# A fused decay-attention and feed-forward kernel: the order of all matmuls written into the source

## The chip, the cores and the metric

One core of a Trainium2 chip runs the whole program. The metric is the device time of one execution in microseconds (us), taken as the median of the runs shown. Engines are named as in the profile: PE is the matrix engine (its weight loads are listed as PEld), DVE the vector engine, ACT the scalar engine, POOL the general one, SP the engine whose queue issues nearly all transfers here.

## The reference: what is computed

A linear attention with a complex decay for each channel, and on its output a two-layer feed-forward net:

```python
mag = np.sqrt(a_re * a_re + a_im * a_im)
scale = np.minimum(mag, 0.999) / (mag + 1e-06)
a_re_n, a_im_n = (a_re * scale, a_im * scale)
for t in range(S):
    new_re = ar * S_re - ai * S_im
    new_im = ar * S_im + ai * S_re
    kv = np.einsum('bhd,bhe->bhde', k[:, :, t], v[:, :, t])
    S_re, S_im = (new_re + kv, new_im)
    y[:, :, t] = np.einsum('bhd,bhde->bhe', q[:, :, t], S_re)
x = y.transpose(0, 2, 1, 3).reshape(B * S, H * D)
h = x @ w_in
out = np.maximum(0.01 * h, h) @ w_out
```

There are 4 batches, 8 heads, 768 positions, a head width of 48; so 3072 tokens of width 384, a hidden width of 2048, all in fp32.

## The kernel before, in words

The sequence is cut into chunks of 128 positions. A **pass** is one chunk of two batches; there are 12 passes (0 to 11), and a pass holds two **units**, one for each batch. The last two passes (10 and 11) are the last chunk of the sequence: they carry no state on and skip the work for it. After each pass its 256 tokens are a **group** (0 to 11) of the feed-forward net.

*Preparing a pass* (`prep`, lines 430 to 603) is DVE and ACT work: the decays are normalised, multiplied up along the chunk (lines 478 to 505), and turned into scaled queries and keys in the tile `qkt`; its last two DVE instructions stand at line 576. Ten transfers on SP's queue (lines 592 to 602) then move `qkt` into the tile `t96` (`t` in the profile). `qkt`, `t96` and the values `v` have one buffer each: the next pass can be moved into `t96` only when the matmuls and scalings that read it for this pass are done.

*Attention of a unit* (`attend`) has these steps on PE. Transposes of the keys (line 635, the tile `kn` after an ACT copy). Scores (line 649), multiplied on DVE with a mask into `asb` (line 657). The output (line 678) from `asb` and `v`, and from the carried state `rst`; ACT and DVE split it into a high and a low part, `xh` and `xl` (lines 680 and 683). The new state (line 692), added on DVE (line 703) and scaled on ACT (line 710, eight instructions). All of them use three PSUM banks in turn.

*The feed-forward net of a group* (`moe`) goes in eight steps of 256 hidden units. Its **first half step** `mm1` is 18 matmuls of 128x256 into the tile `ph` (lines 732 to 734; weights and inputs are split in a high and a low part, and three of the four products are taken). ACT and DVE make the activation and split it: ACT line 738 and DVE line 739 give `tg`, ACT line 740 `gh`, DVE line 741 `gl`. The **second half step** `mm2` is 18 matmuls that add into three tiles `po` (lines 749, 750, 755). `ph` has two buffers, and so have `tg`, `gh` and `gl`. In the source `mm2` of a step stands one step behind `mm1`.

*The weights* arrive as 64-bit words. In the first 156 us they are converted piece by piece on DVE (lines 416 and 420), ACT (423, 425) and POOL (424, 426), 32 pieces, between the preparations of passes 0 to 2. Near the end all weights are read once more and checked on ACT (lines 389 to 396, the tile `wck`).

*What sets the order.* The kernel is written in a framework that records all instructions and, before the program is built, puts those of each engine in one fixed order: it plays the program through with an estimated time for each instruction, and of what is ready takes the one with the lowest priority number. `prio` sets these numbers: attention first, then the feed-forward net, then preparation. So before the change attention and feed-forward matmuls mix on PE as that plan fell out, and the engines then run their lists strictly in order, each instruction waiting for its semaphores.

Of the kernel before, what the change touches and what calls it, by code (L numbers as in the profile page):

```python
# [17 lines left out]
DM = H * D  # L18
# [20 lines left out]
GROUPS = [2] * 12  # L39
GT = max(GROUPS) * C  # L40
GW = max(g * C * max(1, 4 // g) for g in GROUPS)
# [234 lines left out]
def body(ctx, tc, keep, a_in, qk_in, v_in, w_in, out):  # L276
# [23 lines left out]
    wacc = keep.tile([P, 2, WCP * -(-NWC // WCK)], F32, tag="wacc", name="wacc")  # L300

# [314 lines left out]
    def xgroup(u):  # L616
        g = next(g for g in range(len(GROUPS)) if u < sum(GROUPS[: g + 1]))
# [4 lines left out]
        return *xg[g], (u - sum(GROUPS[:g])) * C  # L622

    def attend(n, bi):
        prio(PRIO_ATT)
        c, bs = SUBS[n]
        qkt, t96, v = relay[n]
        for b in bs[bi : bi + 1]:
            xh, xl, x0 = xgroup(SUB_POS[n] // C + bi)
            if c < NCH - 1:  # L630
                kn = pp.tile([P, H, 2, D], F32, tag="kn", name=f"kn_{n}_{bi}")
                for hh in range(2):
                    pt = att_bank()
                    for h4 in range(4):
                        nc.tensor.transpose(  # L635
                            out=pt[:, h4, 0:96],
                            in_=t96[:, slot_of(1, hh * 4 + h4), bi, 0:C],
                            identity=ident[0:96, 0:96],
                        )
                    nc.scalar.copy(  # L640
                        kn[:, hh * 4 : hh * 4 + 4].rearrange("p h l d -> p h (l d)"), pt[:, :, 0:96]
                    )
            am = []
            for hh in range(2):
                ps = att_bank()
                for h4, x in score_order():
                    h = hh * 4 + h4
                    q = block_lane(h4, x)
                    nc.tensor.matmul(  # L649
# [7 lines left out]
                nc.vector.tensor_tensor(  # L657
                    out=asb, in0=ps, in1=mask, op=ALU.mult
                )
                am.append(asb)  # L660
            px = att_bank()
# [14 lines left out]
            for step in zip(*lanes):  # L676
                for q, (i, lhsT, rhs, first, last) in enumerate(step):
                    nc.tensor.matmul(px[32 * q : 32 * q + 32, i], lhsT=lhsT, rhs=rhs, start=first, stop=last)  # L678
            u = SUB_POS[n] // C + bi
# [7 lines left out]
            if c < NCH - 1:  # L687
                pu = att_bank().rearrange("p a b -> p (a b)")
                for h in range(H):
                    o = VW + h * D  # L690
                    for q in range(3):
                        nc.tensor.matmul(
                            pu[32 * q : 32 * q + 32, h * D : (h + 1) * D],
                            lhsT=kn[:, h].rearrange("p l d -> p (l d)")[:, 32 * q : 32 * q + 32],
                            rhs=v[:, bi, o : o + D],
                            start=True,
                            stop=True,
                        )
                u = pu[0:96, 0:DM].rearrange("p (k j e) -> p k j e", j=2, e=D)
                r0 = rst[:, b, 0, 0]  # L700
                r = bass.AP(r0.tensor, r0.offset, [list(r0.ap[0]), [PAIR, H // 2], [64, 2], [1, D]])
                if c > 0:
                    nc.vector.tensor_tensor(out=r, in0=u, in1=r, op=ALU.add)
                src = u if c == 0 else r
                for h0 in (0, 1, 6):
                    hn = 2 if h0 == 6 else 3
                    s0 = slot_of(0, h0)
                    for x in range(hn):
                        h = h0 + (x if h0 == 6 else 2 * x)
                        nc.scalar.activation(  # L710
                            r[:, h // 2, h % 2], src[:, h // 2, h % 2], AF.Copy, scale=t96[:, s0 + x, bi, C : C + 1]
                        )

    def moe(g):
        prio(PRIO_MOE)
        u0 = sum(GROUPS[:g])
        ns = GROUPS[g]
        pos, nt = u0 * C, ns * C
        xh, xl, _ = xgroup(u0)

        po = [pso.tile([P, 512], F32, tag=f"o{o}", name=f"po_{g}_{o}") for o in range(NOC)]

        nf = max(1, 512 // nt)
        w = nf * nt

        def mm1(f0):
            ph = psh.tile([P, 512], F32, tag="h", name=f"ph_{g}_{f0}")
            for f in range(f0, f0 + nf):
                fs = slice(f * P, (f + 1) * P)
                o = ph[:, (f - f0) * nt : (f - f0 + 1) * nt]  # L730
                for k in range(TI):
                    nc.tensor.matmul(o, lhsT=win_hi[:, k, fs], rhs=xh[:, k, :nt], start=(k == 0), stop=False)  # L732
                    nc.tensor.matmul(o, lhsT=win_hi[:, k, fs], rhs=xl[:, k, :nt], start=False, stop=False)  # L733
                    nc.tensor.matmul(o, lhsT=win_lo[:, k, fs], rhs=xh[:, k, :nt], start=False, stop=(k == TI - 1))  # L734
            tg = pp.tile([P, GW], F32, tag="tg", name=f"tg_{g}_{f0}", bufs=2)
            gh = pp.tile([P, GW], F32R, tag="gh", name=f"gh_{g}_{f0}", bufs=2)
            gl = pp.tile([P, GW], F32R, tag="gl", name=f"gl_{g}_{f0}", bufs=2)
            nc.scalar.activation(tg[:, :w], ph[:, :w], AF.Copy, scale=0.01)  # L738
            nc.vector.tensor_tensor(out=tg[:, :w], in0=ph[:, :w], in1=tg[:, :w], op=ALU.max)  # L739
            nc.scalar.copy(gh[:, :w], tg[:, :w])  # L740
            nc.vector.tensor_tensor(out=gl[:, :w], in0=tg[:, :w], in1=gh[:, :w].bitcast(F32), op=ALU.subtract)  # L741
            return gh, gl

        def mm2(f0, gh, gl):
            for f in range(f0, f0 + nf):
                ts = slice((f - f0) * nt, (f - f0 + 1) * nt)
                for o in range(NOC):
                    os = slice(o * P, (o + 1) * P)
                    nc.tensor.matmul(po[o][:, :nt], lhsT=wout_hi[:, f, os], rhs=gh[:, ts], start=(f == 0), stop=False)  # L749
                    nc.tensor.matmul(po[o][:, :nt], lhsT=wout_lo[:, f, os], rhs=gh[:, ts], start=False, stop=False)  # L750
            for f in range(f0, f0 + nf):
                ts = slice((f - f0) * nt, (f - f0 + 1) * nt)
                for o in range(NOC):
                    os = slice(o * P, (o + 1) * P)
                    nc.tensor.matmul(  # L755
                        po[o][:, :nt], lhsT=wout_hi[:, f, os], rhs=gl[:, ts], start=False, stop=(f == NFC - 1)
                    )
# [111 lines left out]
```

## Time and profile before

| what | value |
|---|---|
| median of 3 runs | 689.54 us (688.95 to 689.71) |
| the profiled execution's own time | 694.78 us |
| its span | 692.7 us |
| mean granted clock of PE | 0.959 |
| PE busy | 569.1 us, 82% of the span |
| DVE busy | 550.4 us, 79% |
| ACT busy | 367.4 us, 53% |
| POOL busy | 78.8 us, 11% |

How to read it: the page cuts the span into 40 slices of 17.3 us, with the busy share of each engine in tenths, and the clock that PE was granted. Busy times of PE are modelled ends, so a PE that is shown as busy can still be waiting for a part of that time. A group's row gives the number of its instructions, their summed busy time, the mean of one, and the idle time ahead of them with what ended it. One profiled execution took 5.2 us longer than the median of the runs; all terms of a sum are of that one execution.

### The profile page before, as it was taken

How to read it: one execution, taken by the hardware profiler on the slowest of the kernel's cores; microseconds unless marked ns; L12 is line 12 of the kernel's file. 1: busy time of each engine (PE TensorE's matmuls, PEld its weight loads, DVE VectorE, ACT ScalarE, POOL GpSimd, SP SyncE). 2: the span in 40 equal slices, each digit the busy share in tenths (PEclk: the TensorE clock that was granted, in tenths of full speed). 3: DMA queues.
4: the chain of work that ended last, by engine and by line, in shares of the span. 5: the costliest groups of instructions: out<-in, count | busy, mean ns of one | idle time of the engine just before them, and what ended most of it. 6: DMA issues, size and time to landing. Idle time of an engine off the chain costs nothing.

```text
span 692.7 us, 17741 instructions
## 1 busy us (share of the span) xinstructions
PE 569.1 (82%) x7554; PEld 541.4 (78%) x7554; DVE 550.4 (79%) x917; ACT 367.4 (53%) x827; POOL 78.8 (11%) x75
## 2 busy tenths in 40 slices
PE   1000446999999999999999998999999898799996
PEld 0000335988998899898998998989989888799996
DVE  5999899899979799698897896978979977233332
ACT  6345266358356285283653843836628348584331
POOL 5645355350000000000000000000000000000000
PEclk9999965999999999999999998999999999899999
DMA  9232742722522613416126134170171566870000
GB/s 347 78 102 68 225 146 92 175 102 74 102 84 82 177 51 68 141 53 160 49 68 190 52 70 138 51 185 26 50 206 52 93 234 190 257 261 24 24 1 28
DMA packets 26246, 79.22 MB, mean 114 GB/s; under 512 B 3376, under 2 KB 9520, under 8 KB 26160
## 3 DMA queue, kind: packets, MB, share of 16 engines
q1 hardware_dynamic: 25552, 76.43, 36.7%
q10 hardware_dynamic: 608, 1.59, 1.0%
q8 instruction: 61, 1.00, 0.6%
q14 instruction: 25, 0.20, 0.1%
HBM read 54.26 MB, written 4.72 MB: 85 GB/s over the span
## 4 chain that ended last, share of the span: by engine, by line
DVE 38%; PE 32%; DMA 13%; issue 7%; ACT 4%; SPq 4%; POOL 1%; ACTq 0%; DVEq 0%
DMA t<-qkt 8%; PE po L749 4%; PE ph L734 4%; PE po L750 4%; PE po L755 4%; PE ph L732 4%; PE ph L733 4%; DVE gl L741 3%; PE att L649 3%; DVE tg L739 3%; DMA wck<-in_w_dram 3%; DVE a L530 2%; PE att L678 2%; DVE tmp L481 2%; DVE asb L657 2%
## 5 line engine op out<-in xcount | busy, mean ns | idle before, releaser
L732 PE MATMUL ph<-xh,win_hi 128*128 128x256 f32 x576 | 166.2, 289 | 14.0 <-DVE tg L739 8.6
L733 PE MATMUL ph<-xl,win_hi 128*128 128x256 f32 x576 | 166.4, 289 | 2.6 <-DVE xl L683 2.5
L734 PE MATMUL ph<-xh,win_lo 128*128 128x256 f32 x576 | 165.9, 288 | 0.0
L749 PE MATMUL po<-gh,wout_hi 128*128 128x256 f32 x576 | 147.0, 290 | 1.4 <-ACT gh L740 1.4
L750 PE MATMUL po<-gh,wout_lo 128*128 128x256 f32 x576 | 145.3, 287 | 0.0
L732 PEld LDWEIGHTS ph<-xh,win_hi 128*128 128x128 f32 x576 | 111.4, 194 | 16.3 <-DVE tg L739 10.3
L733 PEld LDWEIGHTS ph<-xl,win_hi 128*128 128x128 f32 x576 | 111.5, 194 | 3.7 <-DVE xl L683 3.1
L749 PEld LDWEIGHTS po<-gh,wout_hi 128*128 128x128 f32 x576 | 111.8, 195 | 3.4 <-ACT gh L740 2.2
L734 PEld LDWEIGHTS ph<-xh,win_lo 128*128 128x128 f32 x576 | 112.1, 195 | 0.5 <-issue 0.4
L750 PEld LDWEIGHTS po<-gh,wout_lo 128*128 128x128 f32 x576 | 111.7, 195 | 0.4
L738 ACT ACTIVATE tg<-ph 128x512 f32<-128x512 f32 x96 | 57.1, 594 | 89.5 <-PE ph L734 79.2
L739 DVE TENSOR_TENSOR tg<-ph,tg 128x512 f32<-128x512 f32 x96 | 65.7, 685 | 48.3 <-ACT tg L738 45.7
L635 PE MATMUL att<-ident,t 96*128 96x96 f32 x160 | 26.9, 272 | 85.5 <-DMA t<-qkt 81.1
L635 PEld LDWEIGHTS att<-ident,t 96*128 96x128 f32 x160 | 16.7, 146 | 94.2 <-DVE a L484 72.5
L755 PE MATMUL po<-gl,wout_hi 128*128 128x256 f32 x576 | 87.5, 286 | 0.2 <-DVE gl L741 0.2
L740 ACT CAST gh<-tg 128x512 fp32r<-128x512 f32 x96 | 59.1, 617 | 48.3 <-DVE tg L739 41.0
L741 DVE TENSOR_TENSOR gl<-tg,gh 128x512 fp32r<-128x512 f32 x96 | 65.8, 688 | 16.4 <-ACT gh L740 14.4
L755 PEld LDWEIGHTS po<-gl,wout_hi 128*128 128x128 f32 x576 | 77.0, 193 | 1.3 <-DVE gl L741 0.4
L657 DVE TENSOR_TENSOR asb<-att,mask 128x512 f32<-128x512 f32 x48 | 32.5, 685 | 39.3 <-PE att L649 39.3
L649 PE MATMUL att<-t 96*32 96x64 f32 (+3 forms) x1536 | 51.6, 267 | 6.0 <-DMA t<-qkt 6.0
L481 DVE TENSOR_TENSOR tmp<-a 128x384 f32<-128x384 f32 x84 | 52.1, 621 | 1.2
L649 PEld LDWEIGHTS att<-t 96*32 96x32 f32 x1536 | 40.2, 147 | 13.9 <-DMA t<-qkt 6.9
(119 smaller groups left out, 938.2 us busy)
## 6 DMA issues: line engine op xcount, KB each, us to landing
t<-qkt SPq DMA_DIRECT2D x44, 290.2 KB, 5.3
wck<-in_w_dram SPq DMA_DIRECT2D x10, 1152.0 KB, 5.6
v<-in_v_dram SPq DMA_DIRECT2D x12, 832.0 KB, 4.4
a<-in_a_dram SPq DMA_DIRECT2D x12, 768.0 KB, 6.1
qk<-in_qk_dram SPq DMA_DIRECT2D x12, 768.0 KB, 4.9
out_dram<-ot SPq DMA_DIRECT2D x12, 384.0 KB, 2.6
stage_xh<-in_w_dram SPq DMA_DIRECT2D x10, 384.0 KB, 3.0
stage_xl<-in_w_dram SPq DMA_DIRECT2D x10, 384.0 KB, 3.6
```

The lines of the kernel that those rows point to most:

```text
L481: nc.vector.tensor_tensor(out=pr, in0=src.unsqueeze(2).to_broadcast([P, 2, 2, M]), in1=swap(ar, r), op=ALU.mult)
L649: nc.tensor.matmul(ps[32 * q : 32 * q + 32, h4].rearrange("p (y x) -> p y x", x=NB)[:, :, x:], lhsT=from_block(t96, 1, h, bi, x, x + 1), r ...
L732: nc.tensor.matmul(o, lhsT=win_hi[:, k, fs], rhs=xh[:, k, :nt], start=(k == 0), stop=False)
L733: nc.tensor.matmul(o, lhsT=win_hi[:, k, fs], rhs=xl[:, k, :nt], start=False, stop=False)
L734: nc.tensor.matmul(o, lhsT=win_lo[:, k, fs], rhs=xh[:, k, :nt], start=False, stop=(k == TI - 1))
L738: nc.scalar.activation(tg[:, :w], ph[:, :w], AF.Copy, scale=0.01)
L739: nc.vector.tensor_tensor(out=tg[:, :w], in0=ph[:, :w], in1=tg[:, :w], op=ALU.max)
L740: nc.scalar.copy(gh[:, :w], tg[:, :w])
L741: nc.vector.tensor_tensor(out=gl[:, :w], in0=tg[:, :w], in1=gh[:, :w].bitcast(F32), op=ALU.subtract)
L749: nc.tensor.matmul(po[o][:, :nt], lhsT=wout_hi[:, f, os], rhs=gh[:, ts], start=(f == 0), stop=False)
L750: nc.tensor.matmul(po[o][:, :nt], lhsT=wout_lo[:, f, os], rhs=gh[:, ts], start=False, stop=False)
L755: nc.tensor.matmul(po[o][:, :nt], lhsT=wout_hi[:, f, os], rhs=gl[:, ts], start=False, stop=(f == NFC - 1))
```

## The change

The matmuls and transposes of attention and of the feed-forward net go through a new helper that tells the framework to keep these instructions on PE in the order of the source. The other engines' orders are still made by the framework.

The order in the source is new. `attend` no longer does its work at once: it returns two pieces for each unit, so four for a pass. The first, `scores`, holds the scores and the first half of the key transposes; the second, `update`, the other half of the transposes, the output and the new state. `moe` is replaced by `first`, `second` and `stream`: `stream` lists the half steps of a group, and `second` of a step now stands two steps behind `first` (after `first` of the step behind next). For groups 2 to 10 the last two `second` half steps are put into the next group's list, behind its `first` of step 0. The main loop walks through the half steps of group n-1 and puts the pieces of pass n between them when few half steps are left (`GAP`, `TAIL`). For passes 1 and 2 `TAIL` is -100, so their four pieces come only when groups 0 and 1 are wholly done. `tg`, `gh` and `gl` get three buffers instead of two.

```diff
+OVERLAP = range(2, 11)
+GAP = 2
+TAIL = [0, -100, -100, 0, 2]
...
+    def mm(out, **kw):
+        tc.keep_in_program_order(nc.tensor.matmul(out, **kw))
...
     def attend(n, bi):
...
+        def turn(hh):
+            pt = att_bank()
...
+            nc.scalar.copy(kn[0][:, hh * 4 : hh * 4 + 4].rearrange("p h l d -> p h (l d)"), pt[:, :, 0:96])
+
+        def scores():
+            prio(PRIO_ATT)
             for hh in range(2):
                 ps = att_bank()
                 for h4, x in score_order():
...
-                    nc.tensor.matmul(
+                    mm(
...
+            if carry:
+                kn.append(pp.tile([P, H, 2, D], F32, tag="kn", name=f"kn_{n}_{bi}"))
+                turn(0)
+
+        def update():
+            prio(PRIO_ATT)
+            if carry:
+                turn(1)
             px = att_bank()
...
+        return [scores, update]
...
-        prev = None
-        for f in range(0, NFC, nf):
-            cur = mm1(f)
-            if prev is not None:
-                mm2(f - nf, *prev)
-            prev = cur
-        mm2(NFC - nf, *prev)
...
+    def first(g, s):
+        prio(PRIO_MOE)
+        xh, xl, _ = xgroup(g * GT // C)
+        ph = psh.tile([P, NF, GT], F32, tag="h", name=f"ph_{g}_{s}")
...
+        tg = pp.tile([P, NF, GT], F32, tag="tg", name=f"tg_{g}_{s}", bufs=3)
+        gh = pp.tile([P, NF, GT], F32R, tag="gh", name=f"gh_{g}_{s}", bufs=3)
+        gl = pp.tile([P, NF, GT], F32R, tag="gl", name=f"gl_{g}_{s}", bufs=3)
...
+    def second(g, s):
...
+    def stream(g):
+
+        late = [(second, g - 1, s) for s in (NS - 2, NS - 1)] if g - 1 in OVERLAP else []
+        order = [(first, g, 0), *late, (first, g, 1), (first, g, 2)]
+        for s in range(3, NS):
+            order += [(second, g, s - 3), (first, g, s)]
+        order += [(second, g, NS - 3)]
+        if g not in OVERLAP:
+            order += [(second, g, s) for s in (NS - 2, NS - 1)]
+        return order
...
+    for n in range(nsub + 1):
+        pieces = []
+        if n < nsub:
+            prep(n, PRIO_PREP + n * 10_000, 1)
...
+            pieces = [p for bi in range(len(SUBS[n][1])) for p in attend(n, bi)]
+        else:
+            check_weights()
+        if n > 0:
+            order = stream(n - 1)
+            for i, (what, g, s) in enumerate(order):
+                what(g, s)
+                left = len(order) - 1 - i
+                while pieces and left <= GAP * len(pieces) + TAIL[min(n, len(TAIL) - 1)]:
+                    pieces.pop(0)()
+                    if left > 0:
+                        break
...
+        for p in pieces:
+            p()
```

**In the program's order, PE, pass 5.** Names with `ph_4_8` belong to group 4 (before the change the second number counts blocks of 128 hidden units, so 8 is step 4; in the changed kernel it counts steps), `asb_5_0_1` is pass 5, unit 0, the second half of the masked scores. Before, in the middle of the first unit:

```order
L678 MATMUL att2_101<-asb_5_0_0_3821,v_5_3112 32x128 x2
L692 MATMUL att0_99<-v_5_3112,kn_5_0_3794 32x48 x24
L755 MATMUL po_4_2_3348<-gl_4_4_3440,wout_hi_75 128x256
L755 MATMUL po_4_0_3346<-gl_4_4_3440,wout_hi_75 128x256
L755 MATMUL po_4_1_3347<-gl_4_4_3440,wout_hi_75 128x256
```

In the changed kernel, the `update` piece of the same unit, between a second and a first half step:

```order
L308 MATMUL po_4_2_3514<-gl_4_1_3481,wout_hi_75 128x256
L647 MATMUL att1_100<-ident_77,t96_5_3374 128x96 x4
L308 MATMUL att2_101<-asb_5_0_0_3549,v_5_2711 32x128 x4
L308 MATMUL att2_101<-t96_5_3374,rst_80 32x128 x4
L308 MATMUL att2_101<-asb_5_0_0_3549,v_5_2711 32x128 x2
L308 MATMUL att2_101<-asb_5_0_1_3567,v_5_2711 32x128 x2
```

Before, the attention of a unit is broken up by single feed-forward matmuls wherever the plan had something ready; now a piece is closed, and it sits behind the second half step of step 1 and ahead of the first half step of step 4.

**In the program's order, DVE, pass 1.** Before, the first masked scores of pass 1 stand between the activations of group 0, in the middle of the conversion of the weights (`wcv`, `stage`):

```order
L739 TENSOR_TENSOR tg_0_8_856<-ph_0_8_837,tg_0_8_856 128x512
L420 SCALAR_TENSOR_TENSOR stage_xh_6_129<-stage_xh_6_129,wcv_29_441 128x384
L416 TENSOR_SCALAR wcv_14_449<-stage_xl_7_130 128x384
L484 TENSOR_TENSOR a_2_1116<-tmp_2_1678 128x2x96
L657 TENSOR_TENSOR asb_1_0_0_1151<-att0_99,mask_78 128x512
L420 SCALAR_TENSOR_TENSOR stage_xl_7_130<-stage_xl_7_130,wcv_14_449 128x384
```

In the changed kernel they stand behind the last `gl` of group 0 and behind half of the preparation of pass 2:

```order
L753 TENSOR_TENSOR tg_0_7_1058<-ph_0_7_1039,tg_0_7_1058 128x512
L533 TENSOR_TENSOR qkt_2_1360<-a_2_756 128x2x768
L469 SCALAR_TENSOR_TENSOR tmp_3_1994<-tmp_3_1994 128x768
L755 TENSOR_TENSOR gl_0_7_1060<-tg_0_7_1058,gh_0_7_1059 128x512
L538 TENSOR_TENSOR a_2_756<-a_2_756 128x1536
L539 TENSOR_TENSOR a_2_756<-a_2_756,qkt_2_1360 128x768
L540 TENSOR_TENSOR a_2_756<-a_2_756,qkt_2_1360 128x768
L475 TENSOR_TENSOR tmp_3_1994<-tmp_3_1994 128x768
L572 TENSOR_TENSOR qkt_2_1360<-qk_2_757,a_2_756 128x6x128
L670 TENSOR_TENSOR asb_1_0_0_1140<-att1_100,mask_78 128x512
```

So the attention of pass 1 moved behind all of group 0 on DVE too. Further on, the second `xl` of pass 1 stands behind the two last instructions of the preparation of pass 2; before, it stood ahead of them, with seven activation instructions of group 1 (four `tg`, three `gl`) in between.

More of the change, by code (lines that the diff above doesn't have):

```diff
@@ L616, in xgroup @@
     def xgroup(u):
-        g = next(g for g in range(len(GROUPS)) if u < sum(GROUPS[: g + 1]))
+        g = u // NGU
         if g not in xg:
@@ L677, in attend @@
                 for q, (i, lhsT, rhs, first, last) in enumerate(step):
-                    nc.tensor.matmul(px[32 * q : 32 * q + 32, i], lhsT=lhsT, rhs=rhs, start=first, stop=last)
-            u = SUB_POS[n] // C + bi
+                    mm(px[32 * q : 32 * q + 32, i], lhsT=lhsT, rhs=rhs, start=first, stop=last)
             nc.scalar.activation(
@@ L686, in attend @@
             )
[L687 to L712, printed above, removed]
@@ L714, in moe @@
-    def moe(g):
-        prio(PRIO_MOE)
[L716 to L757, printed above, removed]
-        prev = None
-        for f in range(0, NFC, nf):
-            cur = mm1(f)
-            if prev is not None:
-                mm2(f - nf, *prev)
-            prev = cur
-        mm2(NFC - nf, *prev)
-        ot = pp.tile([P, NOC, GT], F32, tag="stg", name=f"ot_{g}")
-        for o in range(NOC):
-            nc.scalar.copy(ot[:, o, :nt], po[o][:, :nt])
-        nc.sync.dma_start(out=out[:, :, pos : pos + nt].rearrange("o p t -> p o t"), in_=ot[:, :, :nt])
@@ new lines, in update @@
+            if not carry:
+                return
+            pu = att_bank().rearrange("p a b -> p (a b)")
+            for h in range(H):
+                o = VW + h * D
+                for q in range(3):
+                    mm(
+                        pu[32 * q : 32 * q + 32, h * D : (h + 1) * D],
+                        lhsT=kn[0][:, h].rearrange("p l d -> p (l d)")[:, 32 * q : 32 * q + 32],
+                        rhs=v[:, bi, o : o + D],
+                        start=True,
+                        stop=True,
+                    )
@@ new lines, in update @@
+            new = pu[0:96, 0:DM].rearrange("p (k j e) -> p k j e", j=2, e=D)
+            r0 = rst[:, b, 0, 0]
+            r = bass.AP(r0.tensor, r0.offset, [list(r0.ap[0]), [PAIR, H // 2], [64, 2], [1, D]])
+            if c > 0:
+                nc.vector.tensor_tensor(out=r, in0=new, in1=r, op=ALU.add)
+            src = new if c == 0 else r
+            for h0 in (0, 1, 6):
+                hn = 2 if h0 == 6 else 3
+                s0 = slot_of(0, h0)
+                for x in range(hn):
+                    h = h0 + (x if h0 == 6 else 2 * x)
+                    nc.scalar.activation(
+                        r[:, h // 2, h % 2], src[:, h // 2, h % 2], AF.Copy, scale=t96[:, s0 + x, bi, C : C + 1]
+                    )
@@ L774, in body @@
[L774 to L785 removed]
+    for n in range(nsub + 1):
+        pieces = []
+        if n < nsub:
+            prep(n, PRIO_PREP + n * 10_000, 1)
+            if n + 1 < nsub:
+                load(n + 1)
+            if n == 0:
+                load_weights(EARLY // 2, NFC, PRIO_PREP + 5_000)
+            pieces = [p for bi in range(len(SUBS[n][1])) for p in attend(n, bi)]
[10 more added lines that the diff above has]
+                        break
+                if n == nsub and left == 3:
```

90 lines of the change are left out of this document (52 added, 38 removed).

## The prediction

> **What bounds the kernel now.** First the page: the engines' shares, and the slices of PE, DVE and the clock.
>
> ```profile
> PE 569.1 (82%) x7554; PEld 541.4 (78%) x7554; DVE 550.4 (79%) x917; ACT 367.4 (53%) x827; POOL 78.8 (11%) x75
> PE   1000446999999999999999998999999898799996
> DVE  5999899899979799698897896978979977233332
> PEclk9999965999999999999999998999999999899999
> ```
>
> PE is nearly idle in the first four slices (to 69 us), weak in three more, and then almost full to the end. DVE is full up to about 180 us and has little to do in the last 100. So there are two stages: first DVE, then PE. The stretches show it, and the clock granted in each:
>
> ```profile
> 107.00:181.00 74.00, 66.66 (x717) 62.92 (x718) 71.59 (x111) 42.50 (x99) 23.53 (x20) 0.91 0.33 98
> 181.00:317.00 136.00, 130.80 (x1877) 124.35 (x1876) 118.34 (x203) 75.49 (x181) 0.00 (x0) 0.97 0.35 96
> 317.00:545.00 228.00, 220.23 (x3141) 209.22 (x3141) 199.31 (x343) 126.78 (x303) 0.00 (x0) 0.97 0.35 99
> 545.00:630.00 85.00, 77.23 (x1013) 74.79 (x1013) 48.34 (x97) 53.19 (x100) 0.00 (x0) 0.96 0.72 215
> 630.00:686.00 56.00, 56.00 (x476) 55.84 (x475) 18.05 (x27) 16.81 (x30) 0.00 (x0) 1.00 0.03 9
> ```
>
> After each stretch and its length stand the busy times of PE, PEld, DVE, ACT and POOL, then the clock. From 107 to 181 DVE is busy for 71.59 of 74 us: what it must do sets the pace. From 181 on PE is busy for 96 to 97%, DVE for 87%. PE's work is the same before and after, so what the change can win lies in PE's waits, in time at a reduced clock, and in stalls hidden in the busy time. PE's waits from 177 us to the end:
>
> ```profile
> PE att L635 <- DMA t<-qkt: 7.6, 15, 1.6
> PE att L649 <- DMA t<-qkt: 6.0, 4, 2.7
> PE ph L732 <- DVE tg L739: 5.0, 4, 1.8
> ```
>
> That is 18.6 us, of which 13.6 are attention waiting for `t96`, though feed-forward work was there. The clock cost (1-0.97) x (136+228) + (1-0.96) x 85 = 14.3 us at most.
>
> **The change part by part.** I build the time up from the moment when PE can start group 1.
>
> *The start gets later.* Before, attention of pass 1 filled PE's gaps while group 0 waited for weights and DVE. Now PE does group 0 first, then pass 1. Group 1 needs the second `xl` of pass 1. On DVE this now stands behind the list of work that before ended with the row at 180.85, less the seven activation instructions of group 1 that the order shows:
>
> ```profile
> 178.52 0.68 DVE L741 TENSOR_TENSOR gl<-tg,gh 128x512 fp32r<-128x512 f32 x1
> 179.12 1.82 DVE L576 TENSOR_TENSOR qkt<-qk,a 128x768 f32<-128x768 f32 x2
> 180.85 0.55 DVE L481 TENSOR_TENSOR tmp<-a 128x384 f32<-128x384 f32 x1
> ```
>
> The row at 178.52 is the last of the seven; from start to start it takes DVE 0.60 us. The list ended at 181.3 (180.85 and 0.55, less an overlap of 0.1), less 7 x 0.60 = 177.1. DVE was idle for 2.4 us of the stretch from 107 to 181; I take a quarter of it back: **176.5**. Before, PE had by then done 90 matmuls of group 1 (in the program's order these six are the last of step 0's second half step, behind four first half steps):
>
> ```profile
> 176.02 0.87 PE L755 MATMUL po<-gl,wout_hi 128*128 128x256 f32 x6
> ```
>
> So the change begins with a debt of 90 x 0.1176 = 10.6 us (56 us by 476 instructions in the last stretch is 0.1176 a matmul). Its ends: none, if group 0 and pass 1 were delayed by PE's waits more than by DVE's list, and twice that, if DVE now stands still for PE's scores.
>
> *Group 1, not covered by anything.* 288 x 0.1176 = 33.9 us. Its third first half step needs `ph` back from the first, and ahead of that `tg` DVE has five instructions of line 481 and six of 484:
>
> ```profile
> L481 DVE TENSOR_TENSOR tmp<-a 128x384 f32<-128x384 f32 x84 | 52.1, 621 | 1.2
> L484 DVE TENSOR_TENSOR a<-tmp 128x192 f32<-128x192 f32 x84 | 33.3, 396 | 1.5
> ```
>
> 5 x 0.621 + 6 x 0.396 + 0.69 = 6.2 us against two half steps of 18 x 0.1176 = 2.1 us each: PE waits 2.0 us. Group 1 ends at 176.5 + 33.9 + 2.0 = 212.4.
>
> *A unit of attention on PE.* From closed stretches of the trace:
>
> ```profile
> 250.47 0.43 PE L678 MATMUL att<-asb,v 128*32 128x128 f32 x8
> ...
> 252.26 0.86 PE L692 MATMUL att<-v,kn 128*32 128x48 f32 x48
> 253.04 0.62 PE L755 MATMUL po<-gl,wout_hi 128*128 128x256 f32 x3
> 341.62 1.53 PE L649 MATMUL att<-t 96*32 96x128 f32 x64
> 343.08 0.56 PE L635 MATMUL att<-ident,t 96*128 96x96 f32 x4
> 343.42 0.36 PE L732 MATMUL ph<-xh,win_hi 128*128 128x256 f32 x1
> ```
>
> Scores 1.46, two times four transposes 0.34 each, output 1.79, state 0.78: 4.71 a unit, 9.4 a pass; 6.5 for the last two passes, which have no state. Going in and out of four pieces I put at 0.6 (the matmul at 343.42 and its like hold PE 0.1 to 0.2 longer).
>
> *Pass 2, a closed block.* 9.4 + 0.6, and waits for `asb` and the last `xl` that no feed-forward work covers: at least 0; at most what pass 0 took beyond 9.4, 78.28 to 99.67, which is 12:
>
> ```profile
> 78.28 0.55 PE L635 MATMUL att<-ident,t 96*128 96x96 f32 x2 [72.09 <-DMA t<-qkt]
> ...
> 98.82 0.85 PE L678 MATMUL att<-asb,v 128*32 128x128 f32 x20 [1.49 <-DVE asb L657]
> ```
>
> I take 3, since DVE no longer converts weights there. It ends at 225.4.
>
> *The overlapped part.* Seven groups with full attention: 7 x (33.9 + 9.4 + 0.6) = 307.3. Two with the short one: 2 x 41.0 = 82.0. Group 11 alone: 33.9. The end after PE's last matmul:
>
> ```profile
> 685.73 0.63 PE L755 MATMUL po<-gl,wout_hi 128*128 128x256 f32 x4
> ```
>
> 692.7 - 686.4 = 6.3. Sum: 225.4 + 307.3 + 82.0 + 33.9 + 6.3 = **654.9**, with PE never waiting in its last 430 us. DVE allows it. Two rows of the chain of waits, four passes apart:
>
> ```profile
> 360.17 1.74 DVE qkt L576 x2
> ...
> 543.11 1.81 DVE qkt L576 x2
> ```
>
> 182.9 / 4 = 45.7 us a pass, of which DVE was busy for 199.31/228: 40.0, below 43.9. The slack of the activation is larger than before: `second` two steps behind `first` leaves four half steps, 8.5 us, for two ACT and two DVE instructions. The third buffer costs only memory.
>
> *What stays.* Three items for which the trace of before gives only ends. New waits: 0 to the 18.6 of before; I take 8, the 5.0 for `tg` (ACT and DVE lists are still the plan's) and 3 where the weight check's transfers collide with the last `t96`. Clock: 0 to 14.3; see below, 3. And stalls inside the busy time: the same bricks for before from 177 us (3078 matmuls 362, attention 88, waits 18.6, clock 14.3) make 483 of the 509 us that it took, so 26 are missing. They belong to broken-up attention, where scores and transposes wait for one transfer after another, and closed pieces have fewer of them: 10. Together 21: **675.9** of span.
>
> *The clock.* It is halved after a stretch of 3.4 us that holds transposes and scores and hardly any feed-forward work:
>
> ```profile
> 189.00:192.40 3.40, 2.64 (x41) 1.80 (x39) 1.49 (x4) 1.38 (x3) 0.00 (x0) 1.00 0.96 312
> 192.40:195.80 3.40, 3.40 (x25) 3.27 (x17) 2.46 (x7) 0.40 (x2) 0.00 (x0) 0.51 0.45 186
> ```
>
> In the changed order a `scores` piece is 1.8 us with half steps on both sides, so no such stretch can be without them; passes 1 and 2 are still closed blocks, hence the 3.
>
> The Trainium skill, "TensorE: Matmul & The Clock Gate", Part 1, says that the clock falls to half after a window of about 3.4 us in which PE is idle. Here PE was busy for 2.64 of 3.40 us and was halved all the same, so the trace disagrees; by the rule the closed blocks would cost nothing and the sum would be 3 us less.
>
> **The rivals.** *The reserves aren't needed:* the 21 us fall to about 5, as the bricks say; 660 of span, 657 for the median. For it: PE has no reason left to wait for `t96`. Against: 26 us that the bricks missed in before.
>
> *Nothing won:* in each of the nine overlapped passes PE, now unable to take other work, waits 1.8 us for `asb`, `kn` or `gl` in DVE's and ACT's lists, 16 us more: 692 of span, 689 for the median. Against: four half steps of slack.
>
> *Slower: `t96` comes late in each pass.* It has one buffer, and its transfers must now wait for the end of a pass's fourth piece, after which ten half steps (21.2 us) remain to the next scores. Needed are:
>
> ```profile
> 223.40 1.21 SPq L592 DMA_DIRECT2D t<-qkt  x2
> ...
> 230.11 1.27 SPq L600 DMA_DIRECT2D t<-qkt  x2
> t<-qkt SPq DMA_DIRECT2D x44, 290.2 KB, 5.3
> v<-in_v_dram SPq DMA_DIRECT2D x12, 832.0 KB, 4.4
> L710 ACT ACTIVATE rst<-rst,t 96x48 f32<-96x48 f32 x128 | 30.7, 324 | 2.4 <-DVE rst L703 2.1
> ```
>
> 8 x 0.32 = 2.6 for the scalings that still read it, 8.0 to issue, 5.3 to land: 15.9, and 20.3 if `v`, which now leaves just ahead, takes its 4.4 on top. It decides from 21.2 on. With 3 us more each pass waits 2 to 3 us: 9 x 2.5 = 22 us, 698 of span, 695 for the median.
>
> That the change doesn't do what it says is out: the order on PE shows it.
>
> **How the numbers follow.** Forecast 675.9 + 2.1 (694.78 - 692.7) = 678.0 for the profiled execution, by 689.54/694.78 for the median: **673 us**, 2.4% faster. Chances: the forecast (663 to 685) 0.66, reserves not needed 0.14, nothing won 0.09, slower 0.11. The range reaches to the rivals on both sides, **656 to 691**. A measurement here can tell about 0.2% (1.4 us) from no change: faster 0.83, same 0.05, slower 0.12.
>
> **What would show it.** Right: waits of PE for `t` near 0 from pass 3 on; clock 0.99 or 1.00 from 230 us; group 1 starting at 175 to 179; the last group's output 34 us behind the one before it, with DVE's busy slices reaching into the last 60 us. Wrong: a start of group 1 past 185; waits of `att` for `t` once a pass (the slower rival); PE's idle time ended by DVE or ACT in each pass (nothing won); or a pass of 46 us with no wait shown, which would say that the missing 26 us belong to the bricks themselves.

## The result: slower, 710.2 us against 689.6

The changed kernel takes 710.2 us (706.6 to 711.8), the kernel before 689.6 us on the same chip: a ratio of 1.029, 95% interval 1.025 to 1.033. Forecast were 673 us and faster, with a range of 656 to 691. The profiled execution has a span of 710.0 us, 34.1 us more than the 675.9 that the sum gave, and 17.3 us more than that of the kernel before. Each ratio, here and below, compares fast runs alone, with the kernel before run again beside it, and need not be the quotient of two medians.

The page of the changed kernel, its engines and the slices (17.75 us each):

```profile
PE 563.7 (79%) x7554; PEld 542.9 (76%) x7554; DVE 550.4 (78%) x917; ACT 366.2 (52%) x827; POOL 79.2 (11%) x75
PE   1000448966979889899899998998999979879996
DVE  5999899999799599699896997969969767233331
PEclk9999956967989999999999999999999998989999
```

The work is the same as before (DVE 550.4 us in both), but PE's row is no longer full in the middle, where the forecast had it never wait. The stretches, with the columns of the prediction's table (length, busy time of PE, PEld, DVE, ACT, POOL, then the clock):

```profile
178.00:221.00 43.00, 37.97 (x305) 37.15 (x299) 36.78 (x64) 20.80 (x44) 0.00 (x0) 0.90 0.37 94
317.00:545.00 228.00, 219.47 (x3172) 214.01 (x3172) 197.49 (x343) 125.91 (x299) 0.00 (x0) 0.99 0.35 99
```

Where the time went is told by the moments at which the feed-forward groups are done (the ends of their last matmuls in the traces, in us):

| group done | 1 | 3 | 9 | 11 |
|---|---|---|---|---|
| before | 219.8 | 318.7 | 620.1 | 686.4 |
| changed | 221.4 | 338.2 | 623.4 | 703.6 |

From group 1 to 3 the change loses 17.9 us (116.8 against 98.9). From 3 to 9 it wins 16.2 (47.5 us a group against 50.2, where the forecast had 43.9). In the last two groups it loses 13.9: pass 11's attention, which before was over at 617.7, now lies between their half steps (6.5 us, which are thus only moved out of the stretch before), and a wait of 3.8 us and a clock of 0.96 (3.2 us of the 80.2) come on top. With the 1.6 of group 1 that makes the 17.2.

In the middle DVE is busy for only 197.5 us of 228, and is still in the way. What PE and DVE waited for from 235 to 545 us (total, number of times, longest):

```profile
PE ph L308 <- DVE tg L753: 10.3, 6, 2.4
PE att L647 <- DVE asb L670: 3.5, 2, 3.2
PE att L308 <- DVE asb L670: 3.3, 2, 1.8
...
DVE qkt L533 <- DMA t<-qkt: 26.6, 6, 5.2
DVE qkt L533 <- DMA out_dram<-ot: 6.5, 1, 6.5
```

PE no longer waits for `t96` at all. It waits for DVE, and DVE stands still once a pass, always at the same instruction: line 533, the first that writes into `qkt` for the next preparation. (The output transfer in the last row only came last by the profile; it is the same place.) `qkt` has one buffer, and its old contents must first have been moved into `t96`; `t96` has one buffer too, and can only be filled when the last attention piece of the pass before has been worked off.

One turn of this can be read in order of time, from the changed kernel's timelines of PE, ACT, SP's queue and DVE (start, duration, instruction; in brackets the idle time ahead of it and what ended it). The last piece belongs to pass 5, the transfers to pass 6, line 533 to the preparation of pass 7:

```profile
370.42 0.86 PE L308 MATMUL att<-v,kn 128*32 128x48 f32 x48
...
372.60 1.92 ACT L729 ACTIVATE rst<-rst,t 96x48 f32<-96x48 f32 x8 [1.35 <-DVE rst L722]
...
374.55 1.21 SPq L600 DMA_DIRECT2D t<-qkt  x2
...
381.15 1.26 SPq L608 DMA_DIRECT2D t<-qkt  x2
...
383.09 0.58 ACT L752 ACTIVATE tg<-ph 128x512 f32<-128x512 f32 x1
...
381.09 0.20 DVE L513 TENSOR_TENSOR xs<-tmp 128x48 f32<-128x48 f32 x1
386.45 1.76 DVE L533 TENSOR_TENSOR qkt<-a 128x1536 f32<-128x1536 f32 x1 [5.16 <-DMA t<-qkt]
388.12 0.95 DVE L469 SCALAR_TENSOR_TENSOR tmp<-tmp 128x768 f32<-128x768 f32 x1
388.99 0.68 DVE L753 TENSOR_TENSOR tg<-ph,tg 128x512 f32<-128x512 f32 x1
...
389.73 0.39 PE L308 MATMUL ph<-xh,win_hi 128*128 128x256 f32 x1 [1.25 <-DVE tg L753]
```

The piece's last matmul ends at 371.3, the scalings that read `t96` at 374.5, and in the same moment the first of the ten transfers goes out; the last goes out at 382.4 and has read `qkt` at 386.4. DVE has worked off all that stands ahead of line 533 by 381.3 and waits 5.16 us. The `tg` of the first half step behind it in the list had its ACT half at 383.7 and runs only at 388.99; PE stops for its `ph`. The preparation of pass 6, whose last two instructions stand in this row, had been over since 365.4:

```profile
363.64 1.81 DVE L584 TENSOR_TENSOR qkt<-qk,a 128x768 f32<-128x768 f32 x2
```

So preparation was early, not late: `qkt` lay ready and could not leave, because attention of the pass before was not done. The Trainium skill, "PSUM — Partial Sum Buffer", section "Engine vs sequencer instructions", calls the vector and scalar engines' queues "strict FIFO". The trace agrees: a `tg` that was ready at 383.7 stood behind a write that was not.

### The profile page after: what moved, and what is told of

Read it like the earlier page. It is cut to its first block, busy times and chain, and to the rows that moved or that the text cites. A ratio compares the mean times of both kernels' runs of the same rounds, so it can differ in the third digit from the quotient of the medians.

```text
span 710.0 us, 17654 instructions
## 1 busy us (share of the span) xinstructions
PE 563.7 (79%) x7554; PEld 542.9 (76%) x7554; DVE 550.4 (78%) x917; ACT 366.2 (52%) x827; POOL 79.2 (11%) x75
## 4 chain that ended last, share of the span: by engine, by line
DVE 41%; DMA 19%; PE 19%; ACT 7%; issue 7%; SPq 5%; POOL 1%; DVEq 0%; ACTq 0%
DMA t<-qkt 12%; PE po L308 8%; PE ph L308 6%; DMA wck<-in_w_dram 5%; PE att L308 4%; DVE tmp L489 3%; DVE gl L755 3%; DVE tg L753 3%; DVE asb L670 3%; DVE a L538 3%; ACT rst L729 2%; DVE a L492 2%; SPq L600 2%; DVE wcv L424 2%; SPq L604 2%
## 5 line engine op out<-in xcount | busy, mean ns | idle before, releaser
L308 PE MATMUL ph<-xh,win_hi 128*128 128x256 f32 x576 | 172.7, 300 | 26.8 <-DVE tg L753 20.0
L308 PE MATMUL po<-gh,wout_hi 128*128 128x256 f32 x576 | 144.0, 285 | 5.9 <-ACT ot L778 3.8
L308 PEld LDWEIGHTS ph<-xl,win_hi 128*128 128x128 f32 x576 | 113.9, 198 | 4.2 <-DVE xl L701 4.2
L308 PE MATMUL att<-t 96*32 96x96 f32 (+3 forms) x1536 | 40.7, 261 | 76.3 <-DMA t<-qkt 73.4
L308 PEld LDWEIGHTS att<-t 96*32 96x32 f32 x1536 | 35.8, 146 | 80.6 <-DVE a L492 72.5
L754 ACT CAST gh<-tg 128x512 fp32r<-128x512 f32 x96 | 59.2, 617 | 53.8 <-DVE tg L753 50.9
L308 PE MATMUL po<-gl,wout_hi 128*128 128x256 f32 x576 | 84.5, 282 | 1.9 <-DVE gl L755 1.6
L755 DVE TENSOR_TENSOR gl<-tg,gh 128x512 fp32r<-128x512 f32 x96 | 68.2, 711 | 22.7 <-ACT gh L754 22.5
L533 DVE TENSOR_TENSOR qkt<-a 128x1536 f32<-128x1536 f32 x12 | 22.4, 1869 | 43.6 <-DMA t<-qkt 36.7
L308 PE MATMUL att<-asb,v 128*32 128x128 f32 x768 | 43.3, 312 | 8.8 <-DVE asb L670 8.6
L729 ACT ACTIVATE rst<-rst,t 96x48 f32<-96x48 f32 x128 | 30.7, 323 | 20.2 <-DVE rst L722 20.1
```

Source lines behind the costliest of these rows:

```text
L308: tc.keep_in_program_order(nc.tensor.matmul(out, **kw))
L533: nc.vector.tensor_tensor(out=tb.rearrange("p l (r m) -> p l r m", r=R), in0=zl.rearrange("p l (r m) -> p l r m", r=R), in1=xt[:, 1].rearr ...
L729: nc.scalar.activation(r[:, h // 2, h % 2], src[:, h // 2, h % 2], AF.Copy, scale=t96[:, s0 + x, bi, C : C + 1])
L754: nc.scalar.copy(gh, tg)
L755: nc.vector.tensor_tensor(out=gl, in0=tg, in1=gh.bitcast(F32), op=ALU.subtract)
```

## The experiments

The sign to follow is one number for each pass n: the start of the last output matmul of pass n-1, less the end of the second instruction of line 584 of pass n. Here, for n = 6, that is 370.33 - 365.46 = +4.9 us. When it is below zero, attention is done first and preparation sets the moment at which `t96` is filled. When it is above, DVE runs into line 533 too early. I call it the **lag**. The runs are called e1 to e14.

### Theory A: the wait at line 533 is the cause

```diff
-        qkt = pp.tile(..., tag="qkt", name=f"qkt_{n}")
+        qkt = pp.tile(..., tag="qkt", name=f"qkt_{n}", bufs=2)
```

(and, to make room, the low part of the second weight matrix reduced to one scratch tile, with line 769 reading `wout_hi`: this kernel leaves out the product with that low part)

> Two buffers for qkt. To make room in the on-chip memory the low part of the second weight matrix is not kept: the 576 matmuls that read it read the high part instead (the conversion still runs and writes to a scratch tile), so the output lacks that small term; the number and shape of all instructions is the same. Theory A (a ring through DVE: the first write into qkt of the pass after next, line 533, waits until t96 of the next pass has been read out of qkt, which waits for the last attention piece of this pass; DVE stands still for 4.9 us a pass and everything behind it in its list, tg and gl among it, with it): DVE's wait at line 533 for the transfer falls from 36.7 us in all to under 6, PE's waits for tg after 235 us from 12.4 to under 4, a pass from 46.9 to about 44.4 us (43.9 of PE work and some rest); over 8 passes -20 us: 688 us (683 to 694). Theory B (PE's fixed order itself costs it, since PE cannot take other work when one input is late; DVE is full anyway): less than 5 us of change, 705 to 712.

Measured (e1): 684.6 us, ratio to the kernel before 0.990 (0.987 to 0.993): inside the range of theory A, outside that of theory B. The stretch from 317 to 545, and DVE's longest wait in it:

```profile
317.00:545.00 228.00, 225.89 (x3310) 220.51 (x3310) 209.89 (x363) 142.74 (x326) 0.00 (x0) 1.00 0.41 116
...
DVE qkt L533 <- ACT a L521: 7.0, 3, 4.7
```

No wait for the transfer is left, PE works through 3310 matmuls where the changed kernel had 3172, and a pass takes 45.2 us from pass 4 to pass 10 (first scores at 288.9 and 560.1) instead of 47.6 (296.0 and 581.8). With its order in the source untouched, the kernel goes from 2.9% slower to 1.0% faster than before. Its lag lies between 12 and 28 us from pass 3 on, so late attention by itself costs nothing; it costs where `qkt` has one buffer. That line 769 reads another operand is not what helps: from 317 to 545 us the `po` matmuls are busy for 93.32 us (738 of them) here and for 93.07 (738) in a kernel below, e4, that reads the low part.

### The dose: pieces earlier and later

```diff
-TAIL = [0, -100, -100, 0, 2]
+TAIL = [0, -100, -100, 2, 4]     # early
+TAIL = [0, -100, -100, 0, 0]     # late
```

> The four pieces of passes 3 to 11 are put two half steps (4.2 us of PE) earlier in the feed-forward list; nothing else. Theory A: the last piece ends 4.2 us earlier, so t96 and qkt come free 4.2 us earlier; DVE's wait at line 533 falls from 4.9 to about 1 us a pass, the period from 46.9 to 44 to 44.5 us: 685 to 695 us in all. Theory B (order itself): the scores meet a t96 that has landed only just before, and PE waits there instead: 705 to 715.

> The opposite dose: the pieces of passes 4 to 11 two half steps later. Theory A: each pass of the ring gets 4.2 us longer less the 0.7 us that DVE could still take back; passes 4 to 9: +20 to +25 us, 730 to 735 us, DVE's wait at line 533 8 to 9 us a pass. Theory B: no change within 5 us, or a little faster, since t96 has longer to land.

Measured: 703.6 us for the early pieces (e2; ratio 1.019, 1.012 to 1.025) and 716.2 us for the late ones (e3; 1.034, 1.027 to 1.042). For the earlier pieces the sign is that of theory A; for the later ones too, but there the interval overlaps that of the changed kernel (1.025 to 1.033). The sizes are a third of what was expected, or less. The early kernel has the same wait at the same place:

```profile
415.49 0.20 DVE L513 TENSOR_TENSOR xs<-tmp 128x48 f32<-128x48 f32 x1
420.62 1.76 DVE L533 TENSOR_TENSOR qkt<-a 128x1536 f32<-128x1536 f32 x1 [4.93 <-DMA t<-qkt]
```

My ring of a length that the position of the pieces sets is refuted. DVE's list is made anew by the framework for each kernel, and line 533 again stands behind work that is used up some 5 us before the data has left. The stall stays; where it hits PE changes (in the early kernel also the second half steps, which wait 7.9 us for `gh`).

### Where the lag comes from: the closed blocks of passes 1 and 2

```diff
-TAIL = [0, -100, -100, 0, 2]
+TAIL = [0, 0, 0, 0, 2]
```

> Passes 1 and 2 too put their pieces between the half steps of groups 0 and 1. If the late start (10.6 us of PE work that before had been done by 177 us) is carried to the end: 698 to 702 us, and group 1 ends at 212 to 216 us instead of 221.4. If the ring through DVE sets the pace from pass 3 on whatever PE has in hand: the gain is gone by the last pass, 705 to 712 us, although group 1 ends earlier.

Measured (e4): 674.9 us, ratio 0.977 (0.971 to 0.984), 35 us faster than the changed kernel. Neither reading of mine had that. The profile of this kernel has three things to show: the stretch; the same place in a pass; and the pass time.

```profile
317.00:545.00 228.00, 226.03 (x3357) 221.48 (x3359) 209.70 (x369) 135.79 (x318) 0.00 (x0) 1.00 0.42 113
...
386.70 0.86 PE L308 MATMUL att<-v,kn 128*32 128x48 f32 x48
...
391.26 1.81 DVE L584 TENSOR_TENSOR qkt<-qk,a 128x768 f32<-128x768 f32 x2
...
410.55 1.75 DVE L533 TENSOR_TENSOR qkt<-a 128x1536 f32<-128x1536 f32 x1
...
364.75 1.52 PE L308 MATMUL att<-t 96*32 96x128 f32 x64
...
497.38 1.53 PE L308 MATMUL att<-t 96*32 96x128 f32 x64
```

Attention of pass 6 ends at 387.6, the preparation of pass 7 at 393.1, so the lag is negative; line 533 runs at 410.55 with no wait. And PE goes through three passes in (497.38 - 364.75) / 3 = 44.2 us each, at a clock of 1.00, where the prediction had 43.9. In the source only the start differs from the changed kernel. Two more kernels closed one of the two blocks each:

```diff
+TAIL = [0, -100, 0, 0, 2]     # pass 1 behind group 0
+TAIL = [0, 0, -100, 0, 2]     # pass 2 behind group 1
```

> Only pass 1 stays a closed block behind group 0; pass 2 has its pieces in group 1. Theory C (run-ahead): in the traces so far DVE stands still at line 533 when the last piece of pass n-1 ends later than the preparation of pass n (line 584), and since DVE needs 41 us a pass and PE 44, once that is so it stays so, and a pass takes 46 to 47 us. Here the last piece of pass 2 should end at 222 to 226 us, the preparation of pass 3 at 221 to 223: so it sets in at pass 3. 693 to 702 us, passes 4 to 9 at 46 to 47 us each, DVE's idle time at line 533 over 20 us. Theory D (a closed block costs only its own uncovered time, 5 to 10 us for this one): 680 to 685 us, passes at 44.2 us.

> Only pass 2 stays a closed block behind group 1; pass 1 has its pieces in group 0. Theory C: its last piece ends at about 225 us against 222 for the preparation of pass 3, so the stall sets in as well: 693 to 702 us, passes at 46 to 47 us. Theory D: the block has 9.4 us of work and 2 to 4 us of waits, no more than the same work costs in pieces but for the waits: 677 to 682 us, passes at 44.2 us.

Measured: 702.2 us (ratio 1.015, 1.012 to 1.018) with pass 1 closed (e5), 708.2 us (1.024, 1.022 to 1.027) with pass 2 closed (e6); for the latter 6 us more than theory C gave. The lag by pass, and the mean pass from 4 to 10, all in us:

| kernel | n=3 | 4 | 5 | 6 | 7 | 8 | 9 | 10 | 11 | mean pass | time |
|---|---|---|---|---|---|---|---|---|---|---|---|
| before | -13.8 | -20.3 | -15.3 | -12.4 | -18.7 | -11.4 | -20.2 | -12.9 | -17.3 | (45.5) | 689.6 |
| changed | 13.5 | 2.9 | 0.5 | 4.9 | 4.6 | 5.2 | 6.4 | 5.4 | 9.1 | 47.6 | 710.2 |
| pass 2 closed (e6) | 9.8 | 0.8 | 1.4 | 4.9 | 4.6 | 5.2 | 6.3 | 5.4 | 8.9 | 47.8 | 708.2 |
| pass 1 closed (e5) | 0.6 | 0.1 | -2.4 | -0.3 | 4.9 | 4.6 | 5.2 | 6.4 | 9.6 | 47.7 | 702.2 |
| none closed (e4) | -8.6 | -10.6 | -10.1 | -9.2 | -6.4 | -5.0 | -2.8 | -0.2 | 2.5 | 44.9 | 674.9 |

(In the kernel before attention goes ahead of the feed-forward net, so its pass says little of PE's pace; its groups took 50.2 us.) The three kernels whose lag at pass 3 is above zero end in the same cycle (e5 later than the others), at 45.5 to 52.0 us a pass. The size of the wait at line 533 does not follow that of the lag: in the changed kernel 13.5 us of lag at n = 3 were followed by a wait of 3.4 us, 0.5 at n = 5 by one of 3.0. The one that starts at -8.6 loses 1 to 3 us of it in most passes, since DVE needs less than PE for a pass, and reaches zero only at the end. So a block at the start costs more than its own few microseconds (theory D): it decides on which side of line 533 all later passes run. DVE's wait there for the transfer from 317 to 545 us, in e5 and in e6:

```profile
DVE qkt L533 <- DMA t<-qkt: 21.1, 4, 6.2
...
DVE qkt L533 <- DMA t<-qkt: 22.9, 5, 5.1
```

### The fixed order by itself

```diff
     def mm(out, **kw):
-        tc.keep_in_program_order(nc.tensor.matmul(out, **kw))
+        nc.tensor.matmul(out, **kw)
```

(and the same for the transposes; once in the kernel with no closed blocks, once in the changed kernel as it is)

> As e4 (pieces of all passes between half steps), but matmuls and transposes are no longer kept in the order of the source on PE: the planner may mix them, with the same priorities, the same three buffers and the same order in the source. If the fixed order is what makes a pass 44.2 us (closed pieces, no wait for t96 on PE): 684 to 692 us, a pass at 45.5 to 46.5 us as in the kernel before. If the buffers or the order of issue in the source do it: 672 to 678 us.

> The changed kernel with one thing undone: matmuls and transposes are no longer kept in the order of the source on PE (passes 1 and 2 still stand behind groups 0 and 1 in the source). Theory C with the fixed order as its first cause (the planner gives attention the lower priority number and pulls passes 1 and 2 forward by itself, so preparation cannot run ahead): the last piece of pass n-1 ends 10 us or more ahead of the preparation of pass n, no stall at line 533, 672 to 682 us. If the order in the source alone keeps the two passes back: 700 us or more.

Measured: 677.2 us (e7, no closed blocks; ratio 0.974, 0.967 to 0.982) and 677.7 us (e9, the changed kernel; 0.982, 0.975 to 0.988). Left free, the planner pulls passes 1 and 2 forward by itself; the lag of the second kernel is -15 to -21 us in all passes from 3 on, and -100 in the table of the source has no effect any more. The waits of PE and of DVE from 181 us, in the changed kernel with a free order:

```profile
PE att L308 <- DMA t<-qkt: 12.4, 18, 2.3
...
DVE asb L670 <- PE att L308: 17.4, 15, 3.0
```

These are the waits of the kernel before: preparation is the late side, and PE meets a `t96` that has just landed. All waits of PE from 181 us on make 15.2 us here, 33.7 in the changed kernel. So the fixed order is not what makes a kernel of this kind fast: e4 and e7 are within their intervals of each other. What it did was to make the order at the start binding.

### What is won against the kernel before, and by what

> The kernel before with three buffers for tg, gh and gl, nothing else. If the third buffer is what makes e4 and e7 15 us faster than the kernel before: 674 to 682 us, PE's waits for tg and the idle time of DVE at line 657 down. If it costs only memory, as the prediction has it: 686 to 693 us.

> As e4, but the second half step of a step stands one step behind the first (one late half step instead of two goes into the next group). Between a first half step and the second that needs its result PE then has one half step, 2.1 us, against 2.6 us for two ACT and two DVE instructions alone: 0.5 us at least for 96 steps, 48 us, and more where DVE's list has preparation in between: 715 to 760 us. If the engines' lists make up for it in part: 685 to 715 us. If two steps are not needed: within 4 us of e4, 671 to 679 us.

The first kernel (e10) changes `bufs=2` to `bufs=3` three times in the kernel before: 692.3 us, ratio 1.001 (0.997 to 1.004); no gain. The second (e11) has, in the kernel of e4,

```diff
-        order = [(first, g, 0), *late, (first, g, 1), (first, g, 2)]
-        for s in range(3, NS):
-            order += [(second, g, s - 3), (first, g, s)]
+        order = [(first, g, 0), *late, (first, g, 1)]
+        for s in range(2, NS):
+            order += [(second, g, s - 2), (first, g, s)]
```

and takes 703.4 us (ratio 1.017, 1.011 to 1.024), 28.5 us more than e4, less than the 48 that I had worked out. That working was wrong in its count: in this order a second half step and a first one, two half steps or 4.2 us, stand between a first half step and its second, not one. Nor is all of the 28.5 us the price of less slack: from pass 7 on the lag is above zero, and DVE stands still at line 533 again (3.0 us at 369.23, 5.4 at 414.27). PE's waits from 181 us on show the place, and that they come in a part of the steps only:

```profile
PE po L308 <- ACT gh L754: 24.8, 12, 5.3
PE po L308 <- DVE gl L755: 7.1, 8, 2.0
```

Two edits, one step behind, and a unit's two pieces put together (`return [lambda: (scores(), update())]`), were then made with a free order:

> As e9 (planner free on PE), with the second half step one step behind the first in the source, as in the kernel before. If standing two steps behind is what makes e9 faster than the kernel before: 686 to 693 us. If the split of a unit in two pieces does it: 674 to 681 us.

> As e9 (planner free on PE), with the two pieces of a unit put together again, so that its masked scores, transposes, output and state are issued in one go as in the kernel before. If the split does it: 686 to 693 us. If standing two steps behind does it: 674 to 681 us.

Measured: 685.0 us (e13, one step behind; ratio 0.990, 0.986 to 0.995) and 674.4 us (e14, pieces put together; 0.973, 0.969 to 0.977). With a free order the split of a unit gives nothing. Standing two steps behind gives some 7 of the 13 to 14 us by which e9 beats the kernel before, though the intervals of e9 and e13 overlap a little; by what the rest comes was not tested (the order of issue in the source differs, and three buffers might give something together with it).

### Two attempts to do better

```diff
-        tb = qkt[:, :, 1].rearrange("p l i b t -> p l (i b t)")[:, :, :N]
+        tb = sq
```

> As e4, and the scratch of the preparation (lines 533 to 576) lies in the first two thirds of tmp instead of in qkt, so that the first write into qkt is line 572, 8 us later in DVE's list. e4 meets the stall only at its end (the last piece of pass 10 ends at 569.1, the preparation of pass 11 at 566.6). Theory C: nothing stands still there any more; 2 to 4 us less than e4: 671 to 673 us. But tmp is now busy until line 576, and the beginning of the next preparation can no longer be laid over it: if DVE needs that overlap, a pass grows by up to 4 us and it gets 690 to 710 us.

Measured (e8): 754.2 us, ratio 1.089 (1.085 to 1.092): far above both expectations. A pass took 51.9 us. PE's and DVE's waits from 235 us on:

```profile
PE att L308 <- DMA t<-qkt: 56.2, 18, 13.0
...
DVE asb L670 <- PE att L308: 45.3, 16, 11.6
```

With `tmp` in use up to line 576, the beginning of the next preparation can't be laid over the end of this one, preparation becomes the late side, and PE waits 56 us for `t96`. By the pass of 44.9 us in e4, the overlap was worth about 7 us a pass, not up to 4.

```diff
-TAIL = [0, -100, -100, 0, 2]
+TAIL = [0, 0, 0, 0, 2, 2, 2, 2, 2, 4]
```

> As e4, with the pieces of passes 9 to 11 two half steps earlier. By theory C, e4 loses its lead by 2.5 us a pass (last piece of pass n-1 against preparation of pass n: -9.2, -6.4, -5.0, -2.8, -0.2, +2.5 us) and meets the stall only in the last two passes; 4.2 us earlier it does not meet it: 2 to 5 us less than e4, 670 to 673 us. If e4's last waits come from the weight check on ACT instead: 673 to 677 us.

Measured (e12): 675.6 us, ratio 0.976 (0.971 to 0.981); e4 had 0.977. The lag did stay below zero to the end (-3.1, -3.9, -0.8 for n = 9 to 11), and nothing was gained by it, so of the two readings the second holds. Whether it is the weight check that limits the end was not tested.

The best versions are e4, e7, e12 and e14, 2.3% to 2.7% below the kernel before; their intervals overlap, so they can't be told apart.

## Why the prediction was wrong

**The start of group 1** was forecast for 176.5 and came at 178.4. **The closed block of pass 2** was forecast at 13.0 us and took 13.9 (221.34 to 235.26). Both terms held.

**Group 1** was forecast at 35.9 us and took 42.9 (178.41 to 221.34). Here the step that failed shows first, in the preparation of pass 3, on the changed kernel's timelines of DVE and PE:

```profile
196.83 1.76 DVE L533 TENSOR_TENSOR qkt<-a 128x1536 f32<-128x1536 f32 x1 [5.65 <-DMA t<-qkt]
...
201.78 0.58 PE L308 MATMUL ph<-xh,win_hi 128*128 128x256 f32 x1 [3.88 <-DVE tg L753]
```

This wait and one of 1.07 us at the third first half step, where 2.0 had been forecast, are 3.0 us more than the sum had; the clock of 0.90 over the stretch above is another 4.3 us at most. Together they make up the 7 us.

**The overlapped part.** The bricks were right: with DVE out of the way PE needs 44.2 us a pass (e4), 43.9 in the forecast. The step that failed is the sentence "DVE allows it", with 40.0 us of DVE work against 43.9 of PE work. I took an engine that needs less time for one that can't hold up the other. But it runs ahead until a buffer stops it, and then it stops in the middle of a fixed list in which the activations of the feed-forward net stand behind the blocked write. The trace of before could not show it in a row, since its lag was -11 to -20 us; it could be worked out, though: I had the delay of attention behind preparation in the terms for the start, and did not carry it on to `qkt`. What the runs showed in place of that step: from 235 to 545 us DVE stood still for 33.1 us at line 533, PE waited for 17.3 us behind it, and a pass took 47.6 us; with a second buffer for `qkt` it took 45.2.

**The debt at the start** was put at 10.6 us, once and for all. Of the 34.1 us above the forecast, 9.9 had come up by the end of pass 2 (235.3 against 225.4) and 24.2 after it, beyond the 21 that were held in reserve. Taking the closed blocks away gave 35 us: in e4 group 3 is done at 314.2 and group 9 at 584.4, 24.0 and 39.0 us ahead of the changed kernel. How much of that is the blocks' own cost, e1 tells, which keeps the blocks and has no stall: on the same chip it took 684.6 us against 674.9 of e4. So some 10 us are the blocks' own, close to the 10.6 of the forecast, and some 25 are the stall that they bring on; by group 3, which e1 has done at 327.3, the stall had already cost 10.9 of the 24.0.

**The end.** The forecast had 41.0 us for a light pass and 33.9 for the last group. From the scores of pass 10 to those of pass 11 it took 53.8 (581.8 to 635.6), with four waits of PE that make 9.5 us and a clock of 0.89. The row for the longest wait, and ACT's beside it:

```profile
631.45 0.58 PE L308 MATMUL po<-gh,wout_hi 128*128 128x256 f32 x1 [3.78 <-ACT ot L778]
...
629.84 1.21 ACT L403 ACTIVATE wck<-wck 128x1152 f32<-128x1152 f32 x1 [6.90 <-DMA wck<-in_w_dram]
```

ACT stood 6.9 us at the weight check with the copy of a finished group (`ot`) behind it, which PE needs to begin the next. The reserve had 3 us for such collisions, and put them at `t96`. No run took the check away.

**The reserve.** PE's waits from 178 us to the end made 33.7 us; the sum had 13 (2.0 in group 1, 3 in pass 2, 8 in reserve). The clock was halved for 35.4 us after 178.4, at most 17.7 us lost; the sum had 3. The stalls hidden in the busy time did shrink, as the sum had it. Attention's matmuls from 317 to 545 us (busy time, number, then the clock), before and changed:

```profile
317.00:545.00 228.00, 60.02 (x1840) 0.97 0.35 99
317.00:545.00 228.00, 50.56 (x1772) 0.99 0.35 99
```

So of the 34.1 us above the forecast 1.9 are the later start, 20.7 are waits and at most 14.7 the clock. That makes 37.3, or 3.2 too much: the hidden stalls came to less than the 10 us left in the sum for them, or part of the halved clock fell on an idle PE. Two readings ahead of the sum were off, without weight in it: from 545 to 630 us PE was busy for 91% (77.23 of 85), not 96 to 97, and the 18.6 us of waits are the three largest rows of 20.3.

**The rival "slower"** had the right resource and the right chain: one buffer for `t96`, kept until the fourth piece ends, then 15.9 to 20.3 us until it is filled; measured were 15.2 from the end of the piece (371.3) to the last read (386.4). It gave 22 us in all. Wrong were the place and the point from which it decides. I looked for the wait at the next scores, on PE, from 21.2 us on; there it never came. It came at the source of the transfer, on DVE, and from a lag of about zero on: in the turn above a lag of 4.9 us came with a wait of 5.16, in e4 one of -0.2 with a wait of 3.3. It had 0.11.

**The signs.** "Waits of PE for `t` near 0 from pass 3 on" came true and proved nothing. The clock, 0.99 or 1.00 from 230 us on if right, was 0.97. "PE's idle time ended by DVE or ACT in each pass", the sign of the rival "nothing won", was the one that spoke. Its 16 us of such waits in nine passes are near the 17.3 from 235 to 545; it had the four half steps of slack against it, and no line 533.

**What gains.** The prediction gave the gain to the fixed order and its closed pieces. e7, e9 and e14 have it with neither: with a free order other matmuls stand within the pieces again (in e7, 12 of them between the transposes at 377.42 and the output at 379.30). That the third buffer alone gains nothing held (e10). That four half steps of slack are worth something is what e11 and e13 point to, with the reservations above.

## What to carry to other kernels

A faster engine off the critical path was not harmless here: with single buffers and a strict list it ran ahead to the first write that it might not yet make, and held back what others waited for behind it. Before an order is made binding, work out for each buffer with one copy which side is late, the one that fills it or the one that empties it, and by how much; a delay at the start moved that number for every later round here. And when a wait names an engine, look at what that engine itself stood waiting for, and at which line.

## What was not expected of the hardware

A pause of two microseconds on PE can cost nearly as much again. In the changed kernel, behind a stop at line 533 of 5.17 us, PE waited once for 2.13 us; the stretch with that wait and the next one:

```profile
480.10:483.50 3.40, 1.26 (x11) 1.06 (x10) 3.40 (x4) 0.74 (x1) 0.00 (x0) 1.00 0.00 0
483.50:486.90 3.40, 3.40 (x17) 3.40 (x18) 3.40 (x4) 3.40 (x9) 0.00 (x0) 0.51 0.29 101
```

PE was busy for 1.26 of 3.40 us, and the clock was 0.51 for the 3.40 us that followed, 1.7 us of work lost. The Trainium skill, "TensorE: Matmul & The Clock Gate", Part 1, has the half clock follow an idle window; this window was not idle, as in the prediction's example. A wait of 1.83 us ahead of 436.40 had no such sequel. All changes of the clock in this trace lie whole steps of 3.41 us apart; on that grid the wait of 2.13 us falls into one step, and the one of 1.83 us is divided between two (at 435.8). That this is why was not tested. e4, with hardly any waits, had a clock of 1.00 from 181 to 545 us.
